# One load of 128 rows per chunk, another order of loads and stores at a stage's end, and one of a pair's four sums moved from VectorE to GpSimd

## The chip, the cores and the metric

The kernel runs on one core of one Trainium2 chip. The metric is the device time of one execution, in microseconds (us), as a median over several runs. The engines are called PE (TensorE matmul), PEld (its weight load), DVE (VectorE), ACT (ScalarE), POOL (GpSimd) and SP (SyncE, which here only issues transfers). SP and ACT each have a queue from which they start DMA transfers.

## The reference

A long convolution by FFT feeds two dense layers with different activations.

```python
def _attn_ref(x, v, pos_emb, w1, w2):                 # x, v: 2 x 12480 x 128
    h_filt = (np.maximum(pos_emb @ w1, 0.0) @ w2) * np.exp(-0.01 * pos)[:, None]
    Uf = np.fft.rfft(x * v, n=2 * S, axis=1)
    Hf = np.fft.rfft(h_filt, n=2 * S, axis=0)
    return x * np.fft.irfft(Uf * Hf[None], n=2 * S, axis=1)[:, :S]

def _moe_ref(x, w_in, w_out):                         # d_model 128, d_ff 2048
    r = np.maximum(x @ w_in, 0.0)
    return (r * r) @ w_out

def _moe2_ref(x, w_in, w_out):
    h = x @ w_in
    return (h * np.cos(h)) @ w_out
```

## The kernel before

The work runs in three stages, and every engine takes its instructions in the order in which the code issues them; nothing reorders them.

**Stage one** (to about 280 us) multiplies x by v, makes the filter and does the first half of the transform. It goes over 30 chunks `q` of two pairs `(q, i)`, 60 pairs in all. `load(q)` brings a chunk's inputs into one of five slots by two transfers on SP: `posT` (128 rows) for the small network of the filter and `xve` (112 rows) for x, v and the transform's matrix. `mlp1` is that network's first matmul; `prep` forms the product on POOL (L177) and the filter on PE and ACT; it runs up to five pairs ahead. `pair` makes four PE products A (two calls by two r), scales two of them on ACT (`s`, L197), copies a third to `e` (L200), combines them on DVE into two `v` (L204), and forms four sums in the tile `bt`: three on DVE (L207, L208, L209), the fourth on POOL (L210). `store(q)` writes a chunk's `bt` (112 rows) to the scratch tensor `Bs` from ACT's queue. `bt`, `s`, `e` and `v` each have two buffers, so a pair's writers wait for the readers of the pair before the last.

Between the pairs the weights of the two layers are split into a high and a low part: `decode(4)` after every second pair issues half of one of 16 steps. A step is, in order, L99, L100, L102, L103, L105 on DVE (first half), then L107 and L109 on DVE, L110 on ACT, L112 on DVE and L114 on POOL (second half); L116 on POOL, the step's last instruction, is issued at the head of the next step's first half, just before the next L99 and L100. L100 overwrites the tile `w_b` that L116 still reads. So four pairs hold one step, and between pair 5 and pair 53 there are twelve such rounds.

**Stage two** (to about 555 us) goes over 26 groups `g` of four rows. `load2(g)` brings a group from `Bs` on SP's queue, three groups ahead; two spectra, four products, their totals (`total`, L343) and the inverse (`inverse`, `butterfly`) follow, and the result goes to the scratch tensor `Ds`. The first groups are loaded while stage one ends; the stage begins with 16 more pieces of decode on DVE, for which two blocks of weights (`wr`, L84) are loaded behind the first groups in SP's queue.

**Stage three** (the rest) is the last part of the convolution and the two layers, 50 blocks of up to 512 columns; PE sets its pace, and the change doesn't touch it.

Of the kernel before, what the change touches and what calls it, by code (L numbers as in the profile page):

```python
# [12 lines left out]
ALU = mybir.AluOpType  # L13
# [7 lines left out]
N1, N2, HB = 104, 120, 60  # L21
D = 128
NP = 112
NCH, CB = 30, 2
CI = 2
G4 = 4
NG = N1 // G4
# [26 lines left out]
def conv_moe(ctx, tc, t):  # L54
# [69 lines left out]

    conv_st = ExitStack()
    ring = conv_st.enter_context(tc.tile_pool(name="ring", bufs=NB, side="right"))
    Bg = Bs.rearrange("k (p c) e -> p k (c e)", c=2)
    B2 = {}

    def slot(name, pool=ring):  # L130
        return pool.tile([128, SLOT], F32, tag="ld", name=name)

    def load2(g, rows=slice(0, 2 * HB)):
        if g not in B2:
            B2[g] = slot("B2").rearrange("p (k c e) -> p k c e", k=G4, c=2)
        nc.sync.dma_start(out=B2[g][rows].rearrange("p k c e -> p k (c e)"), in_=Bg[rows, G4 * g:G4 * (g + 1), :])


    with ExitStack() as st:
        c1 = st.enter_context(tc.tile_pool(name="c1", bufs=1))  # L140
        ring1 = st.enter_context(tc.tile_pool(name="ring1", bufs=LDB - NB, side="right"))
        io = st.enter_context(tc.tile_pool(name="io1", bufs=2))
        wk = st.enter_context(tc.tile_pool(name="wk1", bufs=2))
        psA = st.enter_context(tc.tile_pool(name="psA", bufs=6, space=PSUM))
        psM = st.enter_context(tc.tile_pool(name="psM", bufs=1, space=PSUM))

        w1b = c1.tile([128, 128], F32, name="w1b")
        w2b = c1.tile([128, 256], F32, name="w2b")
        win = c1.tile([NP, NCH, CB, 2], F32, name="win")
        tw = c1.tile([NP, 3], F32, name="tw")  # L150
        ld = {}

        def load(q):
            sl = slot("ld", ring if q % LDB < NB else ring1)
            nc.sync.dma_start(out=sl[:, XVE:SLOT0], in_=t["posT"][q])
            nc.sync.dma_start(out=sl[0:NP, 0:XVE], in_=t["xve"][q])
            x, v = (sl[0:NP, 1024 * n:1024 * (n + 1)].rearrange("p (i a d) -> p i a d", i=CB, a=2) for n in range(2))
            et = sl[0:NP, 2048:XVE].rearrange("p (i r k) -> p i r k", i=CB, r=2)
            pt = sl[:, XVE:SLOT0].rearrange("p (i k) -> p i k", i=CB)
            ld[q] = (pt, x, v, et)  # L160

        ut_t, hT_t = {}, {}

        def mlp1(q):
            pt = ld[q][0]
            hp = psM.tile([128, CB, NP], F32, tag="m1", name="hp")
            nc.tensor.matmul(hp, w1b, pt, start=True, stop=True)
            hT = io.tile([128, CB, NP], F32, tag="hT", name="hT", bufs=3)
            nc.scalar.activation(hT, hp, AF.Relu)
            hT_t[q] = hT  # L170

        def prep(q, i):
            _, xt, vt, _ = ld[q]
            if i == 0:
                ut_t[q] = io.tile([NP, CB, 2, 384], F32, tag="ut", name="ut", bufs=3)
            u = ut_t[q]
            nc.gpsimd.tensor_tensor(out=u[:, i, :, 0:256], in0=xt[:, i], in1=vt[:, i], op=ALU.mult)  # L177
            hp = psM.tile([NP, 2, D], F32, tag="m2", name="hp2")
            nc.tensor.matmul(hp, hT_t[q][:, i, :], w2b, start=True, stop=True)
            for a in range(2):  # L180
                nc.scalar.activation(u[:, i, a, 256:384], hp[:, a, :], AF.Copy, scale=win[:, q, i, a:a + 1])

        bt_t = {}

        def pair(q, i):
            if i == 0:
                bt_t[q] = io.tile([NP, CB, 2, 2, 384], F32, tag="bt", name="bt", bufs=2)
            et, u, bt = ld[q][3], ut_t[q], bt_t[q]
            A = {}
            for a in (1, 0):  # L190
                for r in range(2):
                    A[a, r] = psA.tile([NP, 384], F32, tag="A", name="A")
                    nc.tensor.matmul(A[a, r], et[:, i, r, :], u[:, i, a, :], start=True, stop=True)
            s = []
            for r in range(2):
                x = wk.tile([NP, 384], F32, tag=f"s{r}", name=f"s{r}")
                nc.scalar.activation(x, A[1, r], AF.Copy, scale=tw[:, 0:1])  # L197
                s.append(x)
            e = wk.tile([NP, 384], F32, tag="e", name="e")
            nc.scalar.activation(e, A[0, 1], AF.Copy)  # L200
            v = []
            for r in range(2):
                x = wk.tile([NP, 384], F32, tag=f"v{r}", name=f"v{r}")
                nc.vector.scalar_tensor_tensor(out=x, in0=A[1, 1 - r], scalar=tw[:, 2 - r:3 - r], in1=s[r],  # L204
                                               op0=ALU.mult, op1=ALU.add)
                v.append(x)
            nc.vector.tensor_tensor(out=bt[:, i, 0, 0, :], in0=A[0, 0], in1=v[0], op=ALU.add)  # L207
            nc.vector.tensor_tensor(out=bt[:, i, 0, 1, :], in0=A[0, 0], in1=v[0], op=ALU.subtract)  # L208
            nc.vector.tensor_tensor(out=bt[:, i, 1, 0, :], in0=A[0, 1], in1=v[1], op=ALU.add)  # L209
            nc.gpsimd.tensor_tensor(out=bt[:, i, 1, 1, :], in0=e, in1=v[1], op=ALU.subtract)  # L210

        def store(q, rows=slice(0, NP)):
            nc.scalar.dma_start(out=Bs[rows, 8 * q:8 * (q + 1), :].rearrange("k x e -> k (x e)"),
                                in_=bt_t[q][rows].rearrange("k b r c e -> k (b r c e)"))

        nc.vector.memset(w1b, 0.0)
        nc.vector.memset(w2b, 0.0)
        for a in range(2):
            nc.scalar.dma_start(out=w1b[64 * a:64 * a + 64, 64 * a:64 * a + 64], in_=t["w1"])
            nc.scalar.dma_start(out=w2b[64 * a:64 * a + 64, 128 * a:128 * a + 128], in_=t["w2"])  # L220
        nc.scalar.dma_start(out=win, in_=t["win"])
        nc.scalar.dma_start(out=Gt, in_=t["G"])
        nc.scalar.dma_start(out=It, in_=t["IG"])
        nc.scalar.dma_start(out=tw, in_=t["tw"])
        seq = [(q, i) for q in range(NCH) for i in range(CB)]
        done = {"load": 0, "mlp": 0, "prep": 0}

        def upto(kind, fn, n, end):
            while done[kind] < min(n, end):
                fn(done[kind])  # L230
                done[kind] += 1

        upto("load", load, LDB, NCH)
        for n, (q, i) in enumerate(seq):
            lead = min(LA, n + 1) if n else 1
            upto("mlp", mlp1, (n + lead - 1) // CB + 1, NCH)
            upto("prep", lambda m: prep(*seq[m]), n + lead, len(seq))
            pair(q, i)
            upto("mlp", mlp1, (n + lead) // CB + 2 if n else 1, NCH)
            if i == 0 and 0 < q < NCH - 2:  # L240
                store(q - 1)

            if (q, i) == (NCH - 2, 0):
                store(q - 1, slice(0, 16))
                store(q - 1, slice(16, NP))
                load2(0, slice(0, NP))
            if (q, i) == (NCH - 1, 0):
                store(q - 1, slice(0, 16))
                load2(1, slice(0, NP))
            if (q, i) == (NCH - 1, 1):  # L250
                store(q, slice(0, 16))
                load2(0, slice(NP, 2 * HB))
                load2(1, slice(NP, 2 * HB))
                for g in range(2, NB):
                    load2(g)
                store(q - 1, slice(16, NP))
                store(q, slice(16, NP))
            if i == 1:
                upto("load", load, q + LDB + 1, NCH)
            if 2 < n < WS:  # L260
                decode(WRATE[0] if n % WRATE[1] == 0 else 0)
# [19 lines left out]
    with ExitStack() as st:  # L281
# [57 lines left out]
        def total(g, j, c):  # L339
            p1, p2 = pt_t.pop((g, j, c))  # L340
            y = wk.tile([128, 2, 2, D], F32, tag=f"y{c}", name=f"y{c}")
            eng = nc.vector if (j, c) == (0, 0) else nc.gpsimd
            eng.tensor_tensor(out=y, in0=p1, in1=p2, op=ALU.subtract if (j, c) == CROSS else ALU.add)  # L343
            yt[g, j, c] = y

# [349 lines left out]
def host(inp):  # L695
# [6 lines left out]
    for s, d in (("x", "xl"), ("v", "vl")):  # L702
        a = inp[s].reshape(2, N1, 2, NCH, CB, D)
        out[d] = c(pad(a.transpose(3, 1, 4, 2, 0, 5), 1)).reshape(NCH, NP, 1024)
    out["xve"] = np.concatenate([out.pop("xl"), out.pop("vl"), out.pop("E").reshape(NCH, NP, 4 * NP)], 2)
    p = inp["pos_emb"].reshape(N1, 2, NCH, CB, 64)
    out["posT"] = c(pad(p.transpose(2, 1, 4, 3, 0), 4)).reshape(NCH, 128, CB * NP)
    out["w1"] = c(inp["w1"])
    out["w2"] = c(inp["w2"])
    for n in _W:  # L710
# [23 lines left out]
```

## Time and profile before

| what | value |
|---|---|
| three runs | 2865.16, 2858.44, 2862.92 us; median 2862.92 |
| the profiled execution, own time | 2863.99 us |
| its span, first to last instruction | 2862.2 us |
| busy over the span: PE, DVE, ACT, POOL | 96%, 85%, 86%, 49% |
| granted TensorE clock, mean | 0.985 |

The profiled execution's time is 1.8 us more than its span and 1.1 us above the median of the runs. Below, a row of a timeline gives the start in us from the span's start, the length in us, the engine, the line, the operation, the tiles (written `out<-in`) with their shapes, and, in brackets, how long the engine had been idle and what ended that. A row of waits gives who waited for whom, the total in us, the count and the longest. A row of busy time gives the stretch, its length, the busy us of PE, PEld, DVE, ACT and POOL with their counts, the granted clock, the DMA engines' mean busy share and what they moved in GB/s. SPq and ACTq are the two DMA queues; in the rows of queues q1 is SP's and q10 is ACT's.

### The profile page before, as it was taken

Reading aid. Unit: us, or ns where it says so; the run is one execution under the profiler, and the core shown is the slowest. Engines: PE = TensorE matmul, PEld = TensorE weight load, DVE = VectorE, ACT = ScalarE, POOL = GpSimd, SP = SyncE. Lnnn points to the kernel's source line nnn. Section 1 sums busy time; section 2 is a strip of 40 time slices with the busy share of each in tenths; the row PEclk is TensorE's granted clock in tenths of the full one; section 3 lists DMA queues with packets and bytes.
Section 4 is the critical chain, followed back from the end, with each engine's and each line's share of the span. In section 5 each row is a group of like instructions: output and inputs, shape, how many; then the busy total and the mean of one; then the engine's idle time right before and its main releaser. Section 6 shows DMA issues by size and latency. Waiting matters only on the chain.

```text
span 2862.2 us, 39251 instructions
## 1 busy us (share of the span) xinstructions
PE 2754.6 (96%) x11740; PEld 2111.7 (74%) x11740; DVE 2433.8 (85%) x4870; ACT 2454.8 (86%) x4412; POOL 1406.3 (49%) x1112
## 2 busy tenths in 40 slices
PE   7887799899999999999999999999999999999999
PEld 4444234488888888888888888888888888888887
DVE  5888699888888888888888888888888888888888
ACT  4545699689999999999999999999999999999998
POOL 4666588624444444444444444444444444444445
PEclk9999899899999999999999999999999999999999
DMA  9998899610101010100101010101010101011000
GB/s 288 316 324 272 214 272 271 192 39 26 31 27 31 27 31 16 33 28 28 31 27 31 27 31 16 31 27 31 27 31 27 31 16 34 25 31 31 16 8 9
DMA packets 86645, 214.98 MB, mean 75 GB/s; under 512 B 6376, under 2 KB 53952, under 8 KB 79712
## 3 DMA queue, kind: packets, MB, share of 16 engines
q1 hardware_dynamic: 81673, 170.79, 21.6%
q10 hardware_dynamic: 4759, 41.70, 3.7%
q8 instruction: 92, 1.51, 0.2%
q14 instruction: 121, 0.99, 0.1%
HBM read 132.80 MB, written 79.63 MB: 74 GB/s over the span
## 4 chain that ended last, share of the span: by engine, by line
PE 81%; DVE 3%; DMA 2%; ACT 1%; issue 1%; POOL 0%; POOLq 0%; DVEq 0%; ACTq 0%; SPq 0%
PE h L502 13%; PE h L504 12%; PE h L503 12%; PE y L518 12%; PE y L517 12%; PE y L516 12%; PE pc L468 4%; DMA B<-Bs 2%; PE Z L316 1%; PE d L351 1%; PE H L294 1%; DVE dt L366 1%; DVE p L328 0%; DVE hr L308 0%; DVE g L590 0%
## 5 line engine op out<-in xcount | busy, mean ns | idle before, releaser
L607 POOL TENSOR_TENSOR gl<-g,gh 128x512 fp32r<-128x512 f32 (+2 forms) x800 | 1034.2, 1293 | 1265.4 <-ACT gh L598 771.7
L590 DVE TENSOR_TENSOR g<-h,c 128x512 f32<-128x512 f32 (+2 forms) x800 | 537.7, 672 | 245.4 <-ACT c L582 238.2
L502 PE MATMUL h<-zh,wh 128*128 128x512 f32 (+2 forms) x1600 | 642.8, 402 | 0.8 <-DVE zh L486 0.8
L567 ACT ACTIVATE k<-h,quarter 128x512 int32<-128x512 f32 (+2 forms) x800 | 540.9, 676 | 114.6 <-PE h L504 100.4
L518 PE MATMUL y<-gl,wh 128*128 128x512 f32 (+2 forms) x1600 | 624.3, 390 | 3.8 <-POOL gl L607 2.7
L504 PE MATMUL h<-zh,wl 128*128 128x512 f32 (+2 forms) x1600 | 623.6, 390 | 0.0
L503 PE MATMUL h<-zl,wh 128*128 128x512 f32 (+2 forms) x1600 | 623.1, 389 | 0.0
L516 PE MATMUL y<-gh,wl 128*128 128x512 f32 (+2 forms) x1600 | 622.6, 389 | 0.0
L517 PE MATMUL y<-gh,wh 128*128 128x512 f32 (+2 forms) x1600 | 622.0, 389 | 0.0
L582 ACT ACTIVATE c<-r,halfpi 128x512 f32<-128x512 f32 (+2 forms) x800 | 565.1, 706 | 2.6 <-DVE r L575 2.6
L541 ACT ACTIVATE r<-h 128x512 f32<-128x512 f32 (+2 forms) x800 | 471.7, 590 | 89.9 <-PE h L504 89.8
L561 DVE TENSOR_TENSOR gl<-g,gh 128x512 fp32r<-128x512 f32 (+2 forms) x800 | 534.8, 668 | 0.9
L575 DVE CUSTOM_DVE_ANT_0 r<-h,k 128x512 f32<-128x512 f32 (+2 forms) x800 | 533.9, 667 | 0.0
L547 ACT ACTIVATE g<-r 128x512 f32<-128x512 f32 (+2 forms) x800 | 492.5, 616 | 0.6
L554 DVE CAST gh<-g 128x512 fp32r<-128x512 f32 (+2 forms) x800 | 330.1, 413 | 44.4 <-ACT g L547 42.7
L518 PEld LDWEIGHTS y<-gl,wh 128*128 128x128 f32 x1600 | 301.3, 188 | 74.8 <-POOL gl L607 7.7
L504 PEld LDWEIGHTS h<-zh,wl 128*128 128x128 f32 x1600 | 302.1, 189 | 66.7
L516 PEld LDWEIGHTS y<-gh,wl 128*128 128x128 f32 x1600 | 301.7, 189 | 66.9 <-DVE zl L529 0.6
L517 PEld LDWEIGHTS y<-gh,wh 128*128 128x128 f32 x1600 | 301.4, 188 | 66.6
L502 PEld LDWEIGHTS h<-zh,wh 128*128 128x128 f32 x1600 | 302.7, 189 | 58.2 <-issue 1.0
L503 PEld LDWEIGHTS h<-zl,wh 128*128 128x128 f32 x1600 | 302.4, 189 | 56.2
L598 ACT ACTIVATE gh<-g 128x512 fp32r<-128x512 f32 (+2 forms) x400 | 246.1, 615 | 0.1
(67 smaller groups left out, 2622.6 us busy)
## 6 DMA issues: line engine op xcount, KB each, us to landing
Bs<-bt ACTq DMA_DIRECT2D x27, 1344.0 KB
B<-Bs SPq DMA_DIRECT2D x24, 1440.0 KB
ld<-xve SPq DMA_DIRECT2D x30, 1092.0 KB
Ds<-dt SPq DMA_DIRECT2D x26, 960.0 KB
dt<-Ds SPq DMA_DIRECT2D x59, 416.0 KB
xt<-xT SPq DMA_DIRECT2D x60, 208.0 KB
out<-o SPq DMA_DIRECT2D x47, 256.0 KB
tt<-T SPq DMA_DIRECT2D x60, 169.0 KB
```

What stands on the lines that cost most here:

```text
L502: nc.tensor.matmul(h[:, :n], wh[:, f, :], zh[:, :n], start=True, stop=False)
L503: nc.tensor.matmul(h[:, :n], wh[:, f, :], zl[:, :n], start=False, stop=False)
L504: nc.tensor.matmul(h[:, :n], wl[:, f, :], zh[:, :n], start=False, stop=True)
L516: nc.tensor.matmul(y[:, :n], wl[:, f, :], gh[:, :n], start=a, stop=False)
L517: nc.tensor.matmul(y[:, :n], wh[:, f, :], gh[:, :n], start=False, stop=False)
L518: nc.tensor.matmul(y[:, :n], wh[:, f, :], gl[:, :n], start=False, stop=b)
L561: nc.vector.tensor_tensor(out=gl[:, :n], in0=g[:, :n], in1=gh[:, :n].bitcast(F32), op=ALU.subtract)
L567: nc.scalar.activation(k[:, :n], hp[2, u][:, :n], AF.Identity, scale=-1.0, bias=quarter)
L575: nc.vector._custom_dve(TENSOR_ADD_SAT, out=r[:, :n], in0=h[:, :n], in1=k[:, :n], s0=0.25, s1=-0.75)
L582: nc.scalar.activation(c[:, :n], r[:, :n], AF.Sin, bias=halfpi, scale=TWO_PI)
L590: nc.vector.tensor_tensor(out=g[:, :n], in0=h[:, :n], in1=c[:, :n], op=ALU.mult)
L607: nc.gpsimd.tensor_tensor(out=gl[:, :n], in0=g[:, :n], in1=gh[:, :n].bitcast(F32), op=ALU.subtract)
```

## The change

Five things change. (1) A chunk comes by one transfer of 128 rows, `ld`, in which `xve` is padded from 112 to 128 rows and joined with `posT`. (2) A group of stage two is loaded with 128 rows instead of 120; the last eight are never read. (3) At the end of stage one the transfers stand in another order, and the last store is issued from SP. (4) The third sum of a pair goes from DVE, which read A in PSUM, to POOL, which reads the copy `e`. (5) The totals of the last group go from POOL to DVE.

```diff
-    def load2(g, rows=slice(0, 2 * HB)):
+    def load2(g, a=0, b=128):
+
         if g not in B2:
             B2[g] = slot("B2").rearrange("p (k c e) -> p k c e", k=G4, c=2)
-        nc.sync.dma_start(out=B2[g][rows].rearrange("p k c e -> p k (c e)"), in_=Bg[rows, G4 * g:G4 * (g + 1), :])
+        nc.sync.dma_start(out=B2[g][a:b].rearrange("p k c e -> p k (c e)"),
+                          in_=bass.AP(Bs.tensor, G4 * g * 4 * HB * 384 + 768 * a,
+                                      [[768, b - a], [4 * HB * 384, G4], [1, 768]]))
...
-            nc.sync.dma_start(out=sl[:, XVE:SLOT0], in_=t["posT"][q])
-            nc.sync.dma_start(out=sl[0:NP, 0:XVE], in_=t["xve"][q])
+            nc.sync.dma_start(out=sl[:, 0:SLOT0], in_=t["ld"][q])
...
-            nc.vector.tensor_tensor(out=bt[:, i, 1, 0, :], in0=A[0, 1], in1=v[1], op=ALU.add)
+            nc.gpsimd.tensor_tensor(out=bt[:, i, 1, 0, :], in0=e, in1=v[1], op=ALU.add)
             nc.gpsimd.tensor_tensor(out=bt[:, i, 1, 1, :], in0=e, in1=v[1], op=ALU.subtract)
...
             if (q, i) == (NCH - 2, 0):
                 store(q - 1, slice(0, 16))
                 store(q - 1, slice(16, NP))
-                load2(0, slice(0, NP))
+                load2(0, 0, NP)
             if (q, i) == (NCH - 1, 0):
                 store(q - 1, slice(0, 16))
-                load2(1, slice(0, NP))
+                store(q - 1, slice(16, NP))
             if (q, i) == (NCH - 1, 1):
                 store(q, slice(0, 16))
-                load2(0, slice(NP, 2 * HB))
-                load2(1, slice(NP, 2 * HB))
+                load2(0, NP, 2 * HB)
+                load2(1)
+                store(q, slice(16, NP), nc.sync)
                 for g in range(2, NB):
                     load2(g)
-                store(q - 1, slice(16, NP))
-                store(q, slice(16, NP))
...
-            eng = nc.vector if (j, c) == (0, 0) else nc.gpsimd
+            eng = nc.vector if (j, c) == (0, 0) or g == NG - 1 else nc.gpsimd
```

POOL's instructions in stage one, from the L116 of one weight step to the L177 behind the next L114, before (L177 is the product of `prep`, L210 the fourth sum):

```order
L116 TENSOR_TENSOR wl_73<-w_b,w_r 128x512
L177 TENSOR_TENSOR ut<-ld 112x2x256
L210 TENSOR_TENSOR bt<-e,v_1653 112x384
L177 TENSOR_TENSOR ut<-ld 112x2x256
L210 TENSOR_TENSOR bt<-e,v_1689 112x384
L114 TENSOR_TENSOR w_b<-w_a,wh_74 128x512
L177 TENSOR_TENSOR ut<-ld 112x2x256
```

And the same piece of the changed kernel, whose lines stand one lower in the file (L178 is the product, L210 the new third sum, L211 the fourth):

```order
L116 TENSOR_TENSOR wl_73<-w_b,w_r 128x512
L178 TENSOR_TENSOR ut<-ld 112x2x256
L210 TENSOR_TENSOR bt<-e,v_1628 112x384
L211 TENSOR_TENSOR bt<-e,v_1628 112x384
L178 TENSOR_TENSOR ut<-ld 112x2x256
L210 TENSOR_TENSOR bt<-e,v_1663 112x384
L211 TENSOR_TENSOR bt<-e,v_1663 112x384
L114 TENSOR_TENSOR w_b<-w_a,wh_74 128x512
L178 TENSOR_TENSOR ut<-ld 112x2x256
```

Between two products POOL now has two sums where it had one, and L116 and L114 stand behind both.

SP's transfers at the end of stage one, before (the tiles named B are the groups of stage two in their order of loading, 112x4x768 the first 112 rows of one; wr are the weights that the decode at the head of stage two waits for):

```order
L136 DMA B_2170<-Bs 112x4x768
L136 DMA B_2218<-Bs 112x4x768
L136 DMA B_2170<-Bs 8x4x768
L136 DMA B_2218<-Bs 8x4x768
L136 DMA B_2245<-Bs 120x4x768
L84 DMA wr<-moe_w_in 128x1024
L84 DMA wr<-moe_w_out 128x4x256
```

And in the changed kernel:

```order
L136 DMA B_2140<-Bs 112x4x768
L136 DMA B_2140<-Bs 8x4x768
L136 DMA B_2213<-Bs 128x4x768
L214 DMA Bs<-bt 96x3072
L136 DMA B_2216<-Bs 128x4x768
L84 DMA wr<-moe_w_in 128x1024
L84 DMA wr<-moe_w_out 128x4x256
```

The second group's load no longer stands ahead of the first group's last eight rows, it comes in one piece behind them, and the last store has moved from ACT's queue into this one, ahead of the third group and the weights.

## Rows read from the trace of the kernel before

**Rows 1.** Busy time by stretch: span, us, five engines, clock, DMA share, GB/s
```profile
50.00:270.00 220.00, 182.09 (x547) 101.09 (x547) 188.44 (x346) 116.95 (x284) 141.79 (x123) 0.93 0.98 311
320.00:520.00 200.00, 194.83 (x441) 80.01 (x439) 181.72 (x284) 182.34 (x309) 165.61 (x132) 1.00 0.93 264
560.00:2862.00 2302.00, 2293.15 (x10544) 1888.36 (x10544) 1986.61 (x4097) 2093.39 (x3700) 1034.20 (x800) 1.00 0.09 27
```

**Rows 2.** Waits in stage one, 60 to 280 us: total, times, longest
```profile
POOL bt L210 <- DVE v L204: 33.7, 17, 2.5
...
POOL w_b L114 <- DVE w_r L112: 25.9, 11, 2.4
POOL bt L210 <- DMA Bs<-bt: 20.2, 15, 2.7
```

**Rows 3.** POOL's timeline over four pairs: start, us, line, tiles, [idle before]
```profile
147.90 1.00 POOL L210 TENSOR_TENSOR bt<-e,v 112x384 f32<-112x384 f32 x1 [2.25 <-DMA Bs<-bt]
148.85 1.27 POOL L116 TENSOR_TENSOR wl<-w_b,w_r 128x512 fp32r<-128x512 f32 x1
150.08 1.45 POOL L177 TENSOR_TENSOR ut<-ld 112x512 f32<-112x512 f32 x1
154.01 1.00 POOL L210 TENSOR_TENSOR bt<-e,v 112x384 f32<-112x384 f32 x1 [2.48 <-DVE v L204]
...
156.45 1.00 POOL L210 TENSOR_TENSOR bt<-e,v 112x384 f32<-112x384 f32 x1 [0.20 <-DVE v L204]
159.66 1.27 POOL L114 TENSOR_TENSOR w_b<-w_a,wh 128x512 f32<-128x512 f32 x1 [2.21 <-DVE w_r L112]
...
166.00 1.00 POOL L210 TENSOR_TENSOR bt<-e,v 112x384 f32<-112x384 f32 x1 [1.65 <-DMA Bs<-bt]
```

**Rows 4.** DVE's timeline in the same stretch
```profile
149.26 1.14 DVE L99 TENSOR_SCALAR w_a<-wr 128x512 int32<-128x512 int32 x1
150.33 1.48 DVE L100 TENSOR_SCALAR w_b<-wr 128x512 int32<-128x512 int32 x1
...
157.63 0.67 DVE L107 TENSOR_TENSOR w_a<-w_a,w_b 128x512 int32<-128x512 int32 x1
```

**Rows 5.** POOL's timeline: fourth sum of pair 5 and of pair 53
```profile
47.27 1.00 POOL L210 TENSOR_TENSOR bt<-e,v 112x384 f32<-112x384 f32 x1 [5.57 <-DVE v L204]
...
262.57 1.00 POOL L210 TENSOR_TENSOR bt<-e,v 112x384 f32<-112x384 f32 x1 [2.48 <-DVE v L204]
```

**Rows 6.** DMA queues, 50 to 270 us: packets, MB, share of 16 engines
```profile
q1 hardware_dynamic: 10463, 33.89, 59.2%
q10 hardware_dynamic: 3200, 34.41, 38.7%
```

**Rows 7.** Busy time by stretch, handover and start of stage two
```profile
289.00:291.00 2.00, 0.00 (x0) 0.00 (x0) 0.00 (x0) 0.00 (x0) 1.77 (x2) 0.50 1.00 424
306.00:307.00 1.00, 0.27 (x1) 0.00 (x0) 0.00 (x0) 0.96 (x3) 0.73 (x1) 1.00 0.84 273
318.00:323.00 5.00, 5.00 (x11) 2.02 (x11) 3.35 (x5) 4.24 (x8) 3.56 (x4) 0.84 0.99 202
```

**Rows 8.** Timelines of POOL, PE, SP and DVE at the handover
```profile
279.24 0.99 POOL L210 TENSOR_TENSOR bt<-e,v 112x384 f32<-112x384 f32 x1 [1.64 <-DVE v L204]
...
299.26 3.57 PE L294 MATMUL H<-B,Gt 120*128 120x512 f32 x4 [22.43 <-DMA B<-Bs]
...
299.06 0.36 SPq L84 DMA_DIRECT2D wr<-moe_w_in  x1
...
308.88 0.43 DVE L99 TENSOR_SCALAR w_a<-wr 128x512 int32<-128x512 int32 x1 [19.90 <-DMA wr<-moe_w_in]
```

**Rows 9.** Waits in stage two, 320 to 530 us
```profile
PE H L294 <- DMA B<-Bs: 3.4, 8, 0.7
```

**Rows 10.** Chain of work that ended last, end of stage two: start, us, what
```profile
541.40 0.68 DVE y L343
...
551.32 4.48 DMA dt<-dt
```

More of the change, by code (lines that the diff above doesn't have):

```diff
@@ L126, in conv_moe @@
     ring = conv_st.enter_context(tc.tile_pool(name="ring", bufs=NB, side="right"))
-    Bg = Bs.rearrange("k (p c) e -> p k (c e)", c=2)
     B2 = {}
@@ L208, in pair, with store @@
             nc.vector.tensor_tensor(out=bt[:, i, 0, 1, :], in0=A[0, 0], in1=v[0], op=ALU.subtract)
-            nc.vector.tensor_tensor(out=bt[:, i, 1, 0, :], in0=A[0, 1], in1=v[1], op=ALU.add)
+            nc.gpsimd.tensor_tensor(out=bt[:, i, 1, 0, :], in0=e, in1=v[1], op=ALU.add)
             nc.gpsimd.tensor_tensor(out=bt[:, i, 1, 1, :], in0=e, in1=v[1], op=ALU.subtract)
-        def store(q, rows=slice(0, NP)):
-            nc.scalar.dma_start(out=Bs[rows, 8 * q:8 * (q + 1), :].rearrange("k x e -> k (x e)"),
+        def store(q, rows=slice(0, NP), eng=nc.scalar):
+            eng.dma_start(out=Bs[rows, 8 * q:8 * (q + 1), :].rearrange("k x e -> k (x e)"),
                                 in_=bt_t[q][rows].rearrange("k b r c e -> k (b r c e)"))
@@ L704, in host @@
         out[d] = c(pad(a.transpose(3, 1, 4, 2, 0, 5), 1)).reshape(NCH, NP, 1024)
-    out["xve"] = np.concatenate([out.pop("xl"), out.pop("vl"), out.pop("E").reshape(NCH, NP, 4 * NP)], 2)
+    xve = np.concatenate([out.pop("xl"), out.pop("vl"), out.pop("E").reshape(NCH, NP, 4 * NP)], 2)
     p = inp["pos_emb"].reshape(N1, 2, NCH, CB, 64)
-    out["posT"] = c(pad(p.transpose(2, 1, 4, 3, 0), 4)).reshape(NCH, 128, CB * NP)
+    posT = c(pad(p.transpose(2, 1, 4, 3, 0), 4)).reshape(NCH, 128, CB * NP)
+    out["ld"] = np.concatenate([np.pad(xve, [(0, 0), (0, 128 - NP), (0, 0)]), posT], 2)
     out["w1"] = c(inp["w1"])
```

## The prediction

> **What bounds the kernel now.** I read the busy time by stretch first, then the waits of stage one, then two timelines over one round of four pairs, then the queues and the handover. Stage three holds 2302 of the 2862 us, PE is busy in 2293 of them, and no line of it changes [rows 1]; I take it as it is. So everything is decided in the first 560 us. In stage one no engine is full: DVE 188 of 220 us, PE 182, POOL 142, ACT 117, but the DMA engines 0.98 [rows 1]. The reader should not stop at that 0.98. If DMA set the pace, most waits would end on a transfer; POOL's longest waits end on DVE instead (33.7 us on the `v` of L204, 25.9 us on L112), and the wait for a store's landing is 20.2 us of the 220 [rows 2]. One round shows why. At its head POOL finishes a fourth sum at 147.90 and goes on to L116; DVE has L99 and L100 in hand, which take 1.14 and 1.48 us there [rows 3, 4], L100 because it needs L116 done and then finds POOL at work on the product of 150.08. Only then come L102 to L105 and the next `v`, for which POOL stands idle 2.48 us. In the second half L114 waits 2.21 us for L112, and the round ends with 1.65 us for a store [rows 3]. So DVE and POOL wait for each other in turn, and DMA adds a little. From pair 5 to pair 53 twelve rounds took 262.57 - 47.27 = 215.3 us, 17.94 us each [rows 5].
>
> **The moved sum** is the largest term. DVE loses four additions in a round and POOL gains four. A sum on POOL costs 0.95 us, from 147.90 to the next start at 148.85; L116 costs 1.23, to 150.08 [rows 3]. Taking the products at 1.25, POOL's work in a round is now 4 x 0.95 + 4 x 1.25 + 2 x 1.23 = 11.3 us, and its waits 2.48 + 0.20 + 2.21 + 1.65 = 6.5 us; together 17.8, as measured. With four more sums the work is 15.1 us. Which waits stay? The 2.48 stays whole: L100 still can't start before L116, which now stands behind two sums, and POOL has nothing to do until `v` comes. Of the 2.21 one more sum covers 0.95, and DVE gets to L107 sooner; I leave 1.0. The 0.20 and 1.65 are filled. To this comes a new cost: L107, L109 and L112 used to run while POOL was idle, and now POOL has a sum ready then. That such instructions exclude each other with POOL's is what the long L99 and L100 show. L107 alone is 0.67 us [rows 4]; for the three I take 1.1 us, from nothing at the lower end to three times 0.7 = 2.1 at the upper. The round comes to 15.1 + 2.5 + 1.0 + 1.1 = 19.7 us, 1.76 more than now, in twelve rounds 21 us. Bounds: 17.6 (no exclusion, no wait for L112), or -4 us; 20.7 (2.1 for the exclusion), or +33 us. The six pairs behind the last round and those before pair 5 hold no or little decode; I leave them as they are. [...]
>
> **The joined load.** 128 rows of 2720 words are 1.39 MB against 1.23 MB (112 x 2496 and 128 x 224 words), 160 KB more in each chunk. SP's queue moved 33.9 MB in 59.2% of 16 engines' 220 us, 16.3 GB/s per engine, ACT's 34.4 MB in 38.7%, 25.3 GB/s [rows 6]. Some 24.5 chunks fall in this stretch, so SP's queue gets 37.8 MB. At the old rate that is 66% and the sum 105%; at the stores' rate 42% and 81%. For loads of 128 rows the nearest row is the weight blocks of 306 to 307, 273 GB/s at a share of 0.84, so 325 GB/s at a full share, against 202 GB/s for loads of 120 rows and 424 while mostly stores run [rows 7]. At 325 (20 GB/s per engine) the sum is 92%: transfers then end before POOL does, and the term is zero. `mlp1` now waits for the whole chunk where it waited for `posT`, and the matmuls of the next pairs are queued behind it on PE; a load has about a chunk's time, 9 us now and 9.85 by my round, and 1.39 MB beside a store take 8.5 us at 325 GB/s. It just fits; at the old rate it would not (below).
>
> **The handover.** From the last sum (279.24 + 0.99) to the first L99 of stage two (308.88) it takes 28.7 us. PE had its first group at 299.26, but DVE waited 19.9 us for the weights, and these were issued only at 299.06 [rows 8]. In the new order the first group's last rows follow a single small store, then come 1.57 MB, a store of 1.18 MB, 1.57 MB and the weights, 0.52 MB: 4.85 MB. At 325 GB/s that takes 14.9 us, at 424 11.4 us, at 202 24 us. Ahead of it lies the landing of the small store; a small transfer on the final chain took 4.48 us [rows 10], so I allow 5. That gives 20 us in place of 28.7: -9 us. Bounds: 29, or nothing, and 16.4, or -12. What is queued behind the store on SP (the third group, the weights) waits for nothing new, because its sums are done when SP gets there.
>
> **Stage two and the totals.** PE waited 3.4 us in all for groups between 320 and 530 us [rows 9]; faster loads give back at most that, and I take -2 us, the rest being the engines' own pace (ACT 182 and DVE 182 of 200 us [rows 1]). The last group's totals put two additions of 0.68 us [rows 10] on DVE just ahead of the last butterflies, and free d from waiting for POOL; I take +1, between -1 and +2.
>
> **Sum:** 2863.99 + 21 - 9 - 2 + 1 = 2875 us for an execution like the profiled one, which was 1.1 us above its median: 2874.
>
> **The rivals.** *POOL has room.* POOL waits 6.5 us in a round, and the four sums take 3.8; if they all fall into waits, DVE's lighter load and the vanished 1.65 us store wait shorten the round, at best to 16.3 us; I take half, 0.8 us in twelve rounds, -10 us. Time 2864 - 10 - 9 - 2 + 1 - 1 = 2843, own range 2835 to 2853. For it: POOL is busy only 142 of 220 us. Against it: the 2.48 us can't be filled, since POOL's next work hangs on DVE and DVE's on POOL. It decides if the round stays below 17.9.
>
> *Loads of 128 rows are no faster.* Then DMA would need 105% of the old round, 18.8 us, which is still under 19.7, but the store waits would half remain (+0.8 a round: 20.5 us, +31), the handover would give 2 us and stage two nothing: 2864 + 31 - 2 + 1 - 1 = 2893. For it: nothing in the rows shows a load into 128 rows alone for long; against it the 325 GB/s. [...]
>
> **How the numbers follow.** No change that this kernel's runs could tell is within 0.2%, 5.7 us. POOL as the bound has 0.62, with an own range of 2862 to 2888, of which 0.47 is slower, 0.13 within the bound, 0.02 faster. Room on POOL has 0.20, all but 0.01 faster. No faster loads 0.13, slower. For 0.05 I have no story; I give 0.02 to slower, 0.02 to no change and 0.01 to faster. Together slower 0.62, no change 0.16, faster 0.22. The range reaches from 2846 into the first rival to 2889 near the second.
>
> **What would show it.** Rounds on POOL of 19 to 20.5 us, with a POOL that waits little but for `v` behind L116; L100 several us long or late; L107 longer than 0.67. The DMA share of stage one well below 0.98 and hardly a wait on a store. The first L99 of stage two about 20 us behind the last sum. I am wrong if rounds are at or below 17.9, if the DMA share stays near 1, or if the weights still come 28 us behind the last sum.

## The result and the profile after

The changed kernel took 2879.46 us (median of 4 runs, 2877.88 to 2880.62), the kernel before beside it 2860.68 us (4 runs, 2856.42 to 2865.16): ratio 1.0058, 95% interval 1.0044 to 1.0072. It is slower by about 0.6%. Its profiled execution took 2878.9 us with a span of 2877.0 us, 14.8 us more than the span before.

Busy time by stretch, in the columns of [rows 1], for the changed kernel:

```profile
50.00:270.00 220.00, 171.07 (x494) 95.03 (x495) 162.47 (x271) 106.65 (x264) 181.52 (x158) 0.90 0.88 313
340.00:540.00 200.00, 193.15 (x444) 81.07 (x443) 184.83 (x290) 183.83 (x311) 167.51 (x134) 1.00 0.88 281
574.00:2877.00 2303.00, 2293.99 (x10544) 1889.16 (x10544) 1988.15 (x4097) 2093.50 (x3700) 1034.37 (x800) 1.00 0.10 27
```

In stage one POOL went from 142 to 182 us of 220, DVE from 188 to 162, and the DMA share from 0.98 to 0.88 while the GB/s hardly moved. PE fell with the pace of the pairs, 547 matmuls to 494. Stage three is as it was.

The waits of stage one in the changed kernel, 60 to 280 us, answer to [rows 2]:

```profile
DVE w_b L100 <- POOL wl L116: 51.0, 12, 5.2
...
POOL bt L210 <- DVE v L205: 27.4, 11, 2.5
PEld hp L168 <- DMA ld<-ld: 21.2, 12, 3.7
ACT ut L182 <- POOL bt L211: 21.0, 8, 3.0
PE hp L168 <- DMA ld<-ld: 14.3, 9, 3.0
...
POOL w_b L114 <- DVE w_r L112: 9.3, 11, 1.2
```

All three of POOL's waits have shrunk: the one for a store is gone, that for L112 fell from 25.9 to 9.3 us, and that for `v` from 33.7 to 27.4. The longest in the list is new and DVE's: 51.0 us for L116, 12 times. L210 is now the third sum and L211 the fourth. One round on POOL's timeline (the counterpart of [rows 3]):

```profile
144.76 0.99 POOL L210 TENSOR_TENSOR bt<-e,v 112x384 f32<-112x384 f32 x1 [2.49 <-DVE v L205]
145.72 0.99 POOL L211 TENSOR_TENSOR bt<-e,v 112x384 f32<-112x384 f32 x1
...
147.90 1.44 POOL L210 TENSOR_TENSOR bt<-e,v 112x384 f32<-112x384 f32 x1
149.31 1.18 POOL L211 TENSOR_TENSOR bt<-e,v 112x384 f32<-112x384 f32 x1
151.21 1.27 POOL L114 TENSOR_TENSOR w_b<-w_a,wh 128x512 f32<-128x512 f32 x1 [0.72 <-DVE w_r L112]
...
154.62 1.56 POOL L211 TENSOR_TENSOR bt<-e,v 112x384 f32<-112x384 f32 x1
...
159.27 1.27 POOL L116 TENSOR_TENSOR wl<-w_b,w_r 128x512 fp32r<-128x512 f32 x1
160.49 1.27 POOL L178 TENSOR_TENSOR ut<-ld 112x512 f32<-112x512 f32 x1
164.25 1.00 POOL L210 TENSOR_TENSOR bt<-e,v 112x384 f32<-112x384 f32 x1 [2.49 <-DVE v L205]
```

From one third sum behind the 2.49 us wait to the next: 19.49 us. What is left of POOL's idleness is that wait and 0.72 us. L211 at 154.62 and L210 at 147.90 took 1.56 and 1.44 us where such a sum takes 0.99. The reason stands on DVE's timeline of the same round ([rows 4] before):

```profile
147.45 1.04 DVE L107 TENSOR_TENSOR w_a<-w_a,w_b 128x512 int32<-128x512 int32 x1
148.52 1.11 DVE L109 TENSOR_SCALAR w_b<-w_a 128x512 int32<-128x512 int32 x1
149.66 1.37 DVE L112 SCALAR_TENSOR_TENSOR w_r<-w_r,w_b 128x512 f32<-128x512 int32 x1
...
154.93 0.41 DVE L99 TENSOR_SCALAR w_a<-wr 128x512 int32<-128x512 int32 x1
160.57 1.48 DVE L100 TENSOR_SCALAR w_b<-wr 128x512 int32<-128x512 int32 x1 [5.24 <-POOL wl L116]
```

L107 was 0.67 us and is 1.04, and L109 and L112 behind it are stretched further. The three groups in the kernel before, 60 to 260 us (count, busy us, mean ns | idle before):

```profile
L112 DVE SCALAR_TENSOR_TENSOR w_r<-w_r,w_b 128x512 f32<-128x512 int32 x11 | 7.6, 693 | 0.4
L107 DVE TENSOR_TENSOR w_a<-w_a,w_b 128x512 int32<-128x512 int32 x11 | 7.5, 678 | 0.0
L109 DVE TENSOR_SCALAR w_b<-w_a 128x512 int32<-128x512 int32 x11 | 4.7, 426 | 0.4
```

So DVE's lines and POOL's sums take turns. Then L100 stands for 5.24 us until L116 is done.

The first and the last round on POOL in the changed kernel, fourth sums of pair 5 and pair 53, for [rows 5]: (281.51 - 47.66) / 12 = 19.49 us, so this round is an average one.

```profile
47.66 1.00 POOL L211 TENSOR_TENSOR bt<-e,v 112x384 f32<-112x384 f32 x1
...
281.51 0.99 POOL L211 TENSOR_TENSOR bt<-e,v 112x384 f32<-112x384 f32 x1
```

The queues of the changed kernel, 50 to 270 us ([rows 6] before):

```profile
q1 hardware_dynamic: 7605, 37.00, 46.0%
q10 hardware_dynamic: 2944, 31.66, 41.7%
```

SP's queue moved more bytes in less of the engines' time: 37.00 MB in 46.0% of 16 engines' 220 us is 22.8 GB/s per engine, where it was 16.3. The handover of the changed kernel ([rows 8] before):

```profile
299.36 1.44 POOL L211 TENSOR_TENSOR bt<-e,v 112x384 f32<-112x384 f32 x1
...
307.67 0.81 SPq L136 DMA_DIRECT2D B<-Bs  x2
...
309.54 0.79 SPq L84 DMA_DIRECT2D wr<-moe_w_in  x1
...
311.21 3.68 PE L294 MATMUL H<-B,Gt 120*128 120x512 f32 x4 [15.07 <-DMA B<-Bs]
...
323.85 0.43 DVE L99 TENSOR_SCALAR w_a<-wr 128x512 int32<-128x512 int32 x1 [15.68 <-DMA wr<-moe_w_in]
```

The last sum ends at 299.36 + 1.44 = 300.80, SP goes on at 307.67 when the small store has landed, and the weights let L99 go at 323.85: 23.05 us, before 28.65. Last, three marks of the kernel before that were not shown (the first copy of `hr` on DVE; the last `d` on PE; the first matmul of stage three):

```profile
310.56 1.37 DVE L308 COPY hr<-H 64x512 f32<-64x512 f32 x2
...
547.28 1.98 PE L351 MATMUL d<-y,It 128*120 128x512 f32 x4 [1.18 <-POOL y L343]
...
560.39 0.55 PE L502 MATMUL h<-zh,wh 128*128 128x256 f32 x1 [0.79 <-DVE zh L486]
```

The same three on the timelines of the changed kernel:

```profile
325.54 1.37 DVE L308 COPY hr<-H 64x512 f32<-64x512 f32 x2
...
560.10 2.23 PE L351 MATMUL d<-y,It 128*120 128x512 f32 x4 [1.76 <-DVE y L343]
...
574.51 0.55 PE L502 MATMUL h<-zh,wh 128*128 128x256 f32 x1 [0.78 <-DVE zh L486]
```

The span is thus accounted for, in us:

| stretch | before | after | difference |
|---|---|---|---|
| start to the end of the last sum | 280.23 | 300.80 | +20.57 |
| to the first L99 of stage two | 28.65 | 23.05 | -5.60 |
| L99 to the `hr` copy, and on to the last `d` | 238.40 | 236.25 | -2.15 |
| last `d` to the first matmul of stage three | 13.11 | 14.41 | +1.30 |
| to the end of the span | 2301.81 | 2302.49 | +0.68 |

### The profile page after: what moved, and what is told of

The parts are those of the page before. It is cut to its first block, busy times and chain, and to the rows that moved or that the text cites. A ratio compares the mean times of both kernels' runs of the same rounds, so it can differ in the third digit from the quotient of the medians.

```text
span 2877.0 us, 39130 instructions
## 1 busy us (share of the span) xinstructions
PE 2756.0 (96%) x11740; PEld 2114.3 (73%) x11740; DVE 2422.0 (84%) x4813; ACT 2453.4 (85%) x4412; POOL 1469.1 (51%) x1169
## 3 DMA queue, kind: packets, MB, share of 16 engines
q1 hardware_dynamic: 78761, 179.22, 19.6%
## 4 chain that ended last, share of the span: by engine, by line
PE 83%; DVE 3%; ACT 1%; issue 1%; DMA 0%; POOL 0%; POOLq 0%; DVEq 0%; ACTq 0%; SPq 0%
PE h L502 13%; PE h L504 12%; PE h L503 12%; PE y L518 12%; PE y L517 12%; PE y L516 12%; PE pc L468 4%; PE Z L316 2%; PE d L351 2%; PE H L294 1%; DVE hr L308 1%; DVE dt L366 0%; DVE p L328 0%; DVE g L590 0%; ACT k L567 0%
```

## The experiments

The table has all twelve, grouped as below; the ratio is to the kernel before in the same runs, the round is the mean from pair 5 to pair 53 as in [rows 5], and the last two columns are the end of the last sum and the time from there to the first `hr` copy (before: 17.94, 280.23 and 30.33; changed kernel: 19.49, 300.80 and 24.74).

| run | median us | ratio and 95% interval | round | last sum | to `hr` |
|---|---|---|---|---|---|
| e2 third sum on POOL alone | 2884.72 | 1.0081 (1.0067 to 1.0095) | 19.33 | 299.85 | 28.26 |
| e3 joined load alone | 2854.89 | 0.9973 (0.9962 to 0.9984) | 18.01 | 279.79 | 29.94 |
| e4 groups and order alone | 2853.64 | 0.9975 (0.9966 to 0.9984) | 17.64 | 279.87 | 24.90 |
| e1 all but the third sum | 2849.23 | 0.9958 (0.9942 to 0.9974) | 17.34 | 272.65 | 24.89 |
| e6 two loads of 128 rows alone | 2848.55 | 0.9961 (0.9948 to 0.9973) | 16.58 | 261.00 | 30.54 |
| e5 changed, second w_b and w_r | 2876.92 | 1.0056 (1.0043 to 1.0068) | 19.16 | 299.53 | 24.37 |
| e9 as e5, stores on SP | 2878.49 | 1.0061 (1.0047 to 1.0075) | 19.17 | 301.49 | 24.81 |
| e11 changed, stores on SP | 2883.94 | 1.0079 (1.0065 to 1.0092) | 19.39 | 304.71 | 23.87 |
| e7 as e1, weights later | 2852.39 | 0.9968 (0.9955 to 0.9980) | 17.19 | 271.91 | 15.90 |
| e8 as e7, two loads | 2843.08 | 0.9943 (0.9929 to 0.9956) | 16.59 | 263.06 | 16.17 |
| e10 as e8, one third sum in four on POOL | 2848.84 | 0.9957 (0.9943 to 0.9970) | 17.02 | 265.76 | 16.94 |
| e12 as e8, sums against L114 and L116 | 2867.02 | 1.0019 (1.0010 to 1.0029) | 18.44 | 286.59 | 16.14 |

**The parts alone.** Theory 1 was that the third sum on POOL is the whole loss, theory 2 that the joined load is.

e1, against the changed kernel:
```diff
-            nc.gpsimd.tensor_tensor(out=bt[:, i, 1, 0, :], in0=e, in1=v[1], op=ALU.add)
+            nc.vector.tensor_tensor(out=bt[:, i, 1, 0, :], in0=A[0, 1], in1=v[1], op=ALU.add)
```


> The changed kernel with the third sum back on DVE; the joined load, the groups of 128 rows, the new order and the last totals stay. Theory 1, POOL's four extra sums a round (of four pairs) are the whole loss: rounds on POOL fall from 19.49 to 16.3 to 17.3 us, so stage one is at least as short as before, and the handover keeps its 5.6 us: 2840 to 2852 us, faster than both kernels. Theory 2, the joined load is the loss (PE now waits for the whole chunk, 35 us of such waits in 60 to 280 us): rounds stay at 19 or more and the time at 2872 to 2880.

e2, against the kernel before: the same two lines the other way round.

> The kernel before with the third sum alone moved to POOL. Theory 1 (POOL's sums): rounds of 19.4 to 20.5 us instead of 17.94, 18 to 31 us more in stage one and no gain at the handover: 2878 to 2892 us. Theory 2 (the joined load): rounds as before or, with DVE relieved, shorter: 2850 to 2864 us.

e3, against the kernel before (on the host the two inputs are padded and joined):
```diff
-            nc.sync.dma_start(out=sl[:, XVE:SLOT0], in_=t["posT"][q])
-            nc.sync.dma_start(out=sl[0:NP, 0:XVE], in_=t["xve"][q])
+            nc.sync.dma_start(out=sl[:, 0:SLOT0], in_=t["ld"][q])
```


> The kernel before with the joined load of 128 rows alone (posT and xve in one transfer); sums, groups and order as before. Theory 1 with loads of 128 rows as fast as the trace after shows: the store wait of 1.65 us a round goes and the DMA share of stage one falls from 0.98 to 0.85 to 0.92; rounds of 16.3 to 17.3 us, 8 to 20 us less: 2842 to 2855 us. Theory 2 (PE waits for whole chunks): rounds of 18.5 to 19.5 us, 2869 to 2881 us. If loads of 128 rows are no faster than those of 112, 160 KB more in each chunk make it 2868 to 2875 us.

e4, against the kernel before: `load2`, `store` and the three blocks that order them as in the changed kernel, without the joined load, the third sum and the totals.

> The kernel before with the groups of 128 rows and the new order of stores and group loads alone. Rounds as before (17.94 us). The handover, from the last sum to the first L99 of stage two, at 20 to 24 us instead of 28.7, and no wait of PE for a group in stage two (3.4 us before): 2853 to 2860 us. If the handover's gain is given back in stage two, because ACT and DVE bound it: 2860 to 2864 us.

Theory 1 holds. The sum alone costs 23.4 us (2884.72 against 2861.28, 19.33 us a round), and taking it out of the changed kernel makes that faster than before by 12.0 us. Joined load and groups are gains, 6.4 and 7.6 us; the groups give theirs where they were expected, 24.90 us from the last sum to `hr` in place of 30.33, and 234.49 us from `hr` to the last `d` in place of 236.72. But e1 kept rounds of 17.34 us, just beyond the long end of what was expected, and e3's 18.01 us (its profiled execution was 8 us above its median) were not shorter at all and lay in neither theory's range. The waits in e1, 60 to 260 us, say why:

```profile
PEld hp L168 <- DMA ld<-ld: 34.7, 19, 3.9
...
PE hp L168 <- DMA ld<-ld: 22.6, 18, 3.3
```

PE's matmuls wait 22.6 us for the joined load, and its weight loads 34.7 us, largely at the same moments, so that the two can't be added up; for `posT` these had been 4.4 and 10.4 us in the same stretch of the kernel before. Where no such wait falls, rounds in e1 are 16.42 us.

**The load.** e6, against the kernel before (on the host `xve` is padded to 128 rows):
```diff
-            nc.sync.dma_start(out=sl[0:NP, 0:XVE], in_=t["xve"][q])
+            nc.sync.dma_start(out=sl[:, 0:XVE], in_=t["xve"][q])
```


> The kernel before with xve padded to 128 rows but posT still a transfer of its own ahead of it: the bytes and rows of the joined load without the joining. If the joined load gave back part of its gain because mlp1 and the matmuls behind it wait for the whole chunk (63.9 us of waits of PE and its weight loads in 60 to 260 us with the joined load alone): these waits fall below 20 us, rounds at 16.3 to 17.0 us and 2842 to 2851 us. If DVE and POOL bound the round at that point anyway: as with the joined load alone, 2851 to 2858 us. If the gain of the joined load came from one transfer in place of two and not from the 128 rows: 2859 to 2870 us.

The waits for `posT` are gone from the list, rounds are 16.58 us and the time is 12 us below the kernel before, with nothing changed but 16 rows of zeros in each load. SP's queue in e6, 50 to 270 us:

```profile
q1 hardware_dynamic: 11586, 39.43, 52.8%
```

That is 21.2 GB/s per engine against 16.3 [rows 6]: the 128 rows are the gain (why rows make a difference no run here shows), and the joining gives part of it back, 6.3 us between the medians of e3 and e6, whose intervals just overlap; e8 against e7, below, shows 9.3 us for the same edit.

**Why the sum costs what it does.** The forecast's reason was that L100 can't start before L116. e5 takes that away: every other weight block has a second `w_b` and `w_r`.
```diff
...
-        a, b, r = (wt.tile([128, 4, 128], I32, tag=f"w_{n}", name=f"w_{n}") for n in "abr")
+        second = (lambda n: wt2[0] if n != "a" and WORDER.index(step) in (1, 3, 5, 7, 9, 11) else wt)
+        a, b, r = (second(n).tile([128, 4, 128], I32, tag=f"w_{n}", name=f"w_{n}") for n in "abr")
...
```


> The changed kernel, third sum still on POOL, with a second w_b and w_r in stage one, taken by every other weight block, so that L100 and L103 of a block need not wait for L116 of the block before. Theory 1a, the loss is the wait of L100 for L116 (48.0 us in 60 to 260 us, and POOL's 2.49 us a round for the v behind it): that wait goes, rounds fall from 19.49 to 16.5 to 17.5 us, 24 to 36 us less than the changed kernel: 2843 to 2856 us. Theory 1b, the loss is POOL's work itself and its exclusion of DVE's weight lines: POOL was busy 16.1 us of a round, L107, L109 and L112 stay at 1.0 us and more, rounds stay at 18.5 to 19.5 us: 2868 to 2880 us.

Theory 1a, which was mine, falls: the wait for L116 is no longer in the list, and rounds are 19.16 us, in theory 1b's range. What came in its place, on POOL and DVE of e5 in one stretch (in e5's file L101 to L107 are the five lines that were L99 to L105, L213 and L214 the third and the fourth sum):

```profile
154.49 2.92 POOL L214 TENSOR_TENSOR bt<-e,v 112x384 f32<-112x384 f32 x1
154.80 0.41 DVE L101 TENSOR_SCALAR w_a<-wr 128x512 int32<-128x512 int32 x1
...
156.14 0.41 DVE L107 TENSOR_SCALAR w_a<-w_a 128x512 int32<-128x512 int32 x1
```

DVE's five weight lines now run back to back, 154.80 to 156.55, and the fourth sum that POOL had begun beside them takes 2.92 us in place of 0.99: it began 0.31 us ahead of the first of them and ended 0.86 us behind the last. The groups of POOL's instructions in e5, 60 to 260 us, have it on average (busy us, mean ns | idle before):

```profile
L214 POOL TENSOR_TENSOR bt<-e,v 112x384 f32<-112x384 f32 x42 | 55.4, 1319 | 0.0
...
L213 POOL TENSOR_TENSOR bt<-e,v 112x384 f32<-112x384 f32 x41 | 45.9, 1120 | 14.6 <-DVE v L208 7.9 <-DMA Bs<-bt 6.3 <-ACT e L204 0.4
```

The fourth sum is 1319 ns (1143 in the changed kernel, 999 before). POOL's idle time in the stretch went from 34.6 to 23.1 us, its busy time from 170.7 to 183.0: the wait became length. In e5 ACT also waited 22.6 us for the fourth sum, because the store's issue stands in its queue; e9 (with e5's second buffers) and e11 (without) put the stores of stage one on SP's queue.
```diff
-                store(q - 1)
+                store(q - 1, eng=nc.sync)
```


> The changed kernel with the second w_b and w_r of the run before, and with the stores of stage one issued on SP's queue instead of ACT's. With the second buffers alone the wait for L116 was gone but rounds stayed near 19.3 us, and ACT waited 22.6 us in 60 to 260 us for the fourth sum, behind the store's issue in ACT's queue. Theory 1c, the loss is one loop that closes over either wait (L116 to L100, or the fourth sum to the store's issue to ACT's s to v): with both gone rounds fall to 16.5 to 17.5 us, 2843 to 2857 us. Theory 1b, POOL's own work and the mutual exclusion (POOL was busy 196 of 220 us, some 17.3 us a round) bound the round: 18.3 to 19.3 us, 2864 to 2877 us.

> The changed kernel with the stores of stage one on SP's queue, and one w_b and w_r as they are. If ACT's wait for the fourth sum (21.0 us in 60 to 260 us) is on the path: rounds of 17.5 to 18.7 us, 2853 to 2868 us. If L100 behind L116, or POOL's work, bounds the round alone: 19.2 to 19.6 us, 2872 to 2881 us.

Neither shortens a round by more than 0.1 us: 19.17 us against 19.16 in e5, 19.39 against 19.49. Both times lie a little above the second range expected, by 1.5 and 2.9 us. In e11 ACT's wait for the fourth sum fell from 21.0 us to 3.1 and the loss stayed, so it wasn't on the path; theory 1c falls. (In e9 the loads, now behind stores on SP, made PE's matmuls wait 30.6 us, against 12.8 in e5, so it is the weaker evidence.) Last, e12 takes other work off POOL and gives it to DVE, from e8:
```diff
-        nc.gpsimd.tensor_tensor(out=bf, in0=af, in1=wh[:, f].bitcast(F32), op=ALU.subtract)
+        last = nc.vector if n <= 12 else nc.gpsimd
+        last.tensor_tensor(out=bf, in0=af, in1=wh[:, f].bitcast(F32), op=ALU.subtract)
...
-        nc.gpsimd.tensor_tensor(out=wl[:, f], in0=bf, in1=rf, op=ALU.add)
+        last.tensor_tensor(out=wl[:, f], in0=bf, in1=rf, op=ALU.add)
...
-            nc.vector.tensor_tensor(out=bt[:, i, 1, 0, :], in0=A[0, 1], in1=v[1], op=ALU.add)
+            nc.gpsimd.tensor_tensor(out=bt[:, i, 1, 0, :], in0=e, in1=v[1], op=ALU.add)
```


> The kernel with two loads of 128 rows and the weights later, with the third sum on POOL in every pair, and in exchange L114 and L116 of the weight blocks of stage one on DVE. POOL's own work in a round is then 4 x (0.95 + 0.95 + 1.25) = 12.6 us in place of 15.1, and nothing on DVE waits for L116. If POOL's amount of work, and the waits between L112, L114, L116 and L100, made the rounds of 19.5 us: rounds of 15.3 to 16.6 us, where PE and the DMA engines come near their limits, 2830 to 2845 us, at or below the best version so far. If the price is the mutual exclusion of POOL and DVE's weight lines, which are now two more: POOL's sums and products beside them longer than 1.3 us, rounds of 17.5 to 19 us, 2856 to 2875 us.

Nothing waits for L116 there, and rounds are 18.44 us, 1.85 more than in e8 and in the second range expected. Busy time of e12 by stretch:

```profile
50.00:270.00 220.00, 172.46 (x526) 96.40 (x527) 217.13 (x310) 106.44 (x276) 173.23 (x144) 0.95 0.91 318
```

Five groups of DVE's lines in e12, 60 to 260 us (busy us, mean ns | idle before; L207 is `v` there):

```profile
L207 DVE SCALAR_TENSOR_TENSOR v<-A,tw,s 112x384 f32<-112x384 f32 x88 | 49.7, 603 | 0.0
...
L102 DVE TENSOR_SCALAR w_a<-w_a 128x512 f32<-128x512 f32 x11 | 16.3, 1481 | 0.0
L112 DVE SCALAR_TENSOR_TENSOR w_r<-w_r,w_b 128x512 f32<-128x512 int32 x11 | 15.1, 1370 | 0.4
L100 DVE TENSOR_SCALAR w_b<-wr 128x512 int32<-128x512 int32 x11 | 13.4, 1219 | 0.0
...
L103 DVE TENSOR_SCALAR w_r<-wr 128x512 int32<-128x512 int32 x11 | 4.6, 414 | 0.0
```

DVE is busy 217 of 220 us with 310 instructions, where e8's 368 kept it busy for 200 us: L102 and L100 take 1.48 and 1.22 us where L103, also a scalar operation on 128x512 elements, takes 0.41. They alternate with POOL's instructions one by one (in one round DVE starts at 150.09, POOL at 150.99, DVE at 151.24, POOL at 152.13, DVE at 152.38). `v`, which reads PSUM, keeps its 0.60 to 0.61 us (means of 603 ns here, 605 to 609 in both kernels, e1, e5 and e8). So POOL was relieved, but DVE became full, and e12 doesn't tell POOL's amount of work from what the two engines do to each other.

What they do to each other a count shows, over the traces of both kernels and all twelve runs, 60 to 260 us. Of 1253 weight lines on DVE, 605 lie beside an instruction of POOL for more than 0.15 us, and each time one of the two is longer than it is alone (in one case by only 0.08 us). Of the other 648 none is longer. Of the 1560 sums on DVE that lie beside POOL and read one input from PSUM, none is longer either. In the two kernels alone it is 24 of 90 weight lines before and 49 of 85 after that lie beside POOL, without an exception; of the other 102 none is longer, and of the 203 sums on DVE beside POOL none takes more than 0.56 us.

e10 is the small dose, from e8: the third sum on POOL in the pair behind which POOL waits for L112.
```diff
-            nc.vector.tensor_tensor(out=bt[:, i, 1, 0, :], in0=A[0, 1], in1=v[1], op=ALU.add)
+            third, t0 = (nc.gpsimd, e) if (2 * q + i) % 4 == 2 else (nc.vector, A[0, 1])
+            third.tensor_tensor(out=bt[:, i, 1, 0, :], in0=t0, in1=v[1], op=ALU.add)
```


> The kernel with the third sum on DVE, two loads of 128 rows and the weights later, with the third sum on POOL in one pair of four: the pair behind which L114 stands, where POOL waits 2.21 us for L112. If a sum that falls into this wait costs POOL nothing and relieves DVE: rounds fall from 16.43 to 15.8 to 16.2 us, 2835 to 2841 us. If each sum on POOL costs its share of the loss (four cost about 2.4 to 3 us a round): 0.6 to 0.8 us a round more, 2850 to 2853 us. If L112 is only later by the exclusion: equal within 3 us.

POOL's wait for L112 fell to 11.6 us in 60 to 260 us (24.9 in e8), so the sum went where it was meant to go; still the round is 17.02 us against 16.59 and the median 5.8 us more (the intervals overlap). The 0.43 us a round are less than the 0.6 to 0.8 expected of a sum's share, and 2848.84 us lies between the ranges. Even one in four is no gain.

**The handover.** e7, from e1:
```diff
-        decode(WG)
+        decode(WG - 4)
...
+            if n == 3:
+                decode(4)
```


> The changed kernel with the third sum on DVE, and four of the 16 decoding steps at the head of stage two moved behind its fourth product, so that the L99 which waits for the weights stands behind the first hr copy and products on DVE and not ahead of them. If that L99 is what the handover still waits for (PE has its first group 12.6 us ahead of it in the changed kernel): the hr copy comes 8 to 13 us earlier, 2836 to 2843 us. If stage two only waits for its next groups or for the moved steps instead: 2845 to 2850 us.

The first `hr` copy comes 9.0 us sooner after the last sum, as expected, but the run is no faster than e1, and the 2836 to 2843 us expected of it were missed: from `hr` to the last `d` it took 243.46 us in place of 235.68. Of these 7.8 us the moved lines are the largest piece that I can name; DVE's timeline in e7:

```profile
308.46 1.15 DVE L99 TENSOR_SCALAR w_a<-wr 128x512 int32<-128x512 int32 x1
309.52 1.49 DVE L100 TENSOR_SCALAR w_b<-wr 128x512 int32<-128x512 int32 x1
310.93 1.48 DVE L102 TENSOR_SCALAR w_a<-w_a 128x512 f32<-128x512 f32 x1
```

L99 to L105 last from 308.46 to 313.01 there, 4.6 us, against 1.7 us at the handover, where POOL was idle. The rest lies in the first copies of `hr` being further apart and was not followed up. e8 is e7 with `posT` and the padded `xve` as two transfers, as in e6.

> The kernel of the run before this one (third sum on DVE, weights later) with posT and a padded xve as two transfers of 128 rows in place of the joined one. If the wait for the whole chunk still costs there: 3 to 8 us less than that run, 2830 to 2840 us. If the rounds of 16.4 us are bound by DVE and POOL: equal to it within 2 us.

2843.08 us, 0.9943 of the kernel before: the lowest median of all, and faster than both kernels, though its interval overlaps those of e1, e6 and e10. Its gain over e7, 9.3 us where 3 to 8 were expected, is the load's.

## Why the prediction was right, by its steps

It said 2875 us for an execution like the profiled one, which was 2878.9; slower held, and the range did. The difference of 3.9 us is in the terms.

**The moved sum (+21): +20.57 to the last sum.** The twelve rounds gave 18.6 us, the pairs around them 2.0, which had been taken as nothing; that the term comes out within half a microsecond is in part luck. The round was put together rightly, term by term: work 15.1 us (the starts on POOL give 15.0), the wait for `v` 2.5 (2.49), that for L112 1.0 (0.72), exclusion 1.1 (1.3 on POOL). The old round, which the prediction adds up to 17.8 us, was 18.10 us in the rows that it was read from; the product at 150.08, lengthened to 1.45 us beside L100, is most of the difference. On DVE, L107, L109 and L112 had means of 678, 426 and 693 ns and have 926, 1107 and 1168: 1.40 us a round.

What failed is the reason given for the second term, "L100 still can't start before L116": with that dependency cut (e5) the round shortened by 0.3 us, not by 2.5. The wait was the shape that the conflict took in this order of work, not its cause. Shown are that the sum on POOL alone makes the loss (e1, e2), that neither that wait nor the store's issue does (e5, e11), that giving L114 and L116 to DVE in exchange doesn't cure it (e12), and, by the count over the traces, that POOL's instructions and DVE's weight lines exclude each other. That this exclusion is what holds the round near 19 us is the reading that fits all of them and the sum in the last section; no run could switch it off. DVE's lines that read PSUM are not stretched: their means are 603 to 609 ns for `v` and 542 to 549 for the sums in both kernels, e1, e5, e8 and e12. What in the engines makes the one kind of line exclude POOL and the other not, no run here shows.

**The joined load (0).** The DMA share was to fall to some 92% and fell to 0.88, and store waits on POOL are gone. The step "It just fits" failed: PE's matmuls waited 14.3 us for the joined load in the changed kernel, 22.6 and 27.4 where the rounds were shorter (e1, e3). In the changed kernel the rounds were even, at 19.1 to 19.6 us behind a first one of 20.1, and e2, with the old loads, had 19.33, so most of this seems hidden behind POOL; what it cost there stays open, since no run gave that kernel two loads with nothing else changed.

**The handover (-9): -5.60.** Both parts were sized too small: the landing of the small store was allowed 5 us and took 6.87 (300.80 to 307.67), the 4.85 MB behind it were given 14.9 us and took 16.18, 300 GB/s in place of 325.

**Stage two (-2): -2.15**, and e4 shows that it comes with the groups: from the first `hr` to the last `d` the traces with groups of 128 rows have 234.5 to 235.7 us, those with 120 rows 236.1 to 239.8 (e7, e8, e10 and e12, whose weights come later, left out). **The totals (+1): +1.30.** The traces with the totals on DVE (the changed kernel, e1, e5 and e7 to e12) have 14.2 to 14.5 us from the last `d` to stage three, those without (before, e2, e3, e4, e6) 13.1 to 13.2. Stage three, taken as unchanged, took 0.7 us more.

**The rivals.** "POOL has room" would have needed rounds below 17.9; e10 shows that not even a quarter of the sums fits into POOL's waits for free. "Loads of 128 rows are no faster" is refuted by 22.8 and 21.2 GB/s per engine against 16.3 in stage one; and in stage two the DMA share fell with 128 rows from 0.93 to 0.88, at 281 GB/s in place of 264.

## What to carry to other kernels

Before an elementwise operation on SBUF goes from VectorE to an idle-looking GpSimd, see in the trace which VectorE instructions exclude GpSimd's (here the weight lines, which read and write SBUF alone: 605 of 605 beside POOL) and add their time to GpSimd's work: there the two share one budget (18.5 us a round in the sum below, against 19.2 to 19.5 measured), and idle time on GpSimd isn't free (in e10 a sum put where POOL waited for L112 cost 0.43 us a round). A wait that ends on another engine's instruction can be the form of such a conflict; cut the dependency and see whether the time goes or only changes shape (in e5 48.0 us of waits for L116 between 60 and 260 us went, and the round only fell from 19.49 to 19.16 us). Try a load padded to 128 rows where the bytes allow it (12 us here), but keep what is needed first in a transfer of its own (6.3 us between e3 and e6, 9.3 between e7 and e8).

## What was unexpected

Added up, POOL's work of a round (15.0 us) and DVE's eight weight lines at their unstretched lengths (five at 0.34 from start to start, L107 0.67, L109 0.43, L112 0.69: 3.5 us) make 18.5 us, an estimate from the rows above. If the two never run at once, no order of the same instructions gets a round below that, and it is more than the 17.94 us of before. The rounds of the five kernels with all third sums on POOL and the weight lines on their old engines are 19.2 to 19.5; the 0.7 to 1.0 us on top are not accounted for one by one. For e12 it is 4 x (0.95 + 0.95 + 1.22) = 12.5, the 3.5, and two lines more at 0.67 or so each, 17.3 in all, against 18.44. Without the third sums it is 11.2 + 3.5 = 14.7, well below the 16.6 to 18.0 us of before, e1, e3, e4 and e6, which other things bound. And 16 rows of zeros, 160 KB more to move per chunk, were worth 12 us.
